# Order of the attention steps between the matmuls of a feed-forward block

## The chip, the core and the metric

The kernel runs on one core of a Trainium2 chip. The core has five engines that run side by side, each with its own queue of instructions in order: TensorE (matmuls, PE in the profile, its weight loads PEld), VectorE (DVE), ScalarE (ACT), GpSimd (POOL) and SyncE (SP), which issues transfers. Matmuls write to PSUM, an accumulator memory of eight banks of 512 fp32 numbers in each of 128 partitions. The other engines copy from there to SBUF, the working memory.

The metric is the device time of one execution in microseconds (us), as the median of several.

## What is computed

The inputs are q, k and v of shape (4, 8, 768, 64): four batches, eight heads, 768 positions of 64 numbers. A small matrix for each head, normalised by five rounds of exp and of division by its row and column sums, mixes the eight blocks of 96 positions of k and of v. Each block of q then attends to its mixed block, and a gated feed-forward block (FFN) follows on all 3072 tokens.

```
P = sort_net                                   # (4, 8, 8, 8), then 5 rounds:
    P = exp(P - max(P)); P = P / sum(P, -1); P = P / sum(P, -2)
k_sorted = einsum('bhij,bhjcd->bhicd', P, k_b)
v_sorted = einsum('bhij,bhjcd->bhicd', P, v_b)
scores = scale * q_b @ k_sb^T
attn = softmax(scores)
x = (attn @ v_sb)  -> (3072, 512)
g = x @ w_gate;  out = (silu(g) * (x @ w_val)) @ w_out
```

The weights w_gate and w_val are 512 x 1536, and w_out is 1536 x 512.

## The kernel before

**FFN stages.** The tokens are worked in eight half batches n = 0 to 7 of 384 tokens, two to a batch. In a stage, twelve blocks m of 128 hidden columns are computed one after another. `gate(n, m)` (L342) is four matmuls into the tile g_ps; ScalarE takes its tanh (th_sb, L354) and VectorE makes gs_sb of both (L356). `value(n, m)` (L360) is four matmuls into v_ps, which VectorE multiplies by gs_sb into h (L369). `outp(n, t3, part)` (L374) is the out projection of 128 tokens: three parts of four matmuls each into o_ps, then a copy to o_sb on ScalarE (L386) and a store from SyncE (L388). The out projection of stage n runs within stage n + 1, after blocks 3, 7 and 11; that of stage 7 stands at the end of the kernel.

**Attention steps.** They are put between the FFN's matmuls. The work for one unit u (a pair of heads and half of a batch's blocks; eight units to a batch) has these steps:

- `qk(b, u)` (L262): eight matmuls of 64 rows (L275), scores of two heads, into two PSUM banks, and one exp of both on ScalarE (L284) into `e_all`, a ring of eight slots.
- `av(b, u)` (L287): eight matmuls on the values (L295) into two banks. VectorE takes a reciprocal (L299) and scales (L301) into st.
- batches 0 and 1: `xtr` (L315), four transposes on TensorE (L312), and a copy on VectorE (L211) into xt, the input of the FFN; batches 2 and 3: `x_dma` (L323), a transposing transfer from SyncE.

Before the units of a batch its keys and queries are mixed in six chunks by `kq_chunk` (L227; 32 matmuls of 64 columns, L233, and one cast out of PSUM on VectorE or ScalarE, L211 or L213). The values of batch 1 are mixed in four chunks by `v_chunk` (L238; 16 matmuls on the 64 upper rows of vch, L245), and those of batches 2 and 3 together in eight by `v_pair_chunk` (L249; L255). For batches 2 and 3 the keys are mixed together as one pair ("p"), and the queries come by a transfer, `q_dma`.

**PSUM.** There are four tags. "gen" has three single banks, taken in turn by g_ps, v_ps and o_ps. "x" has one bank. "a" and "b" have two banks each: scores go to b, values to a, and chunks to b and a in turn. A tile can be taken only when the last reader of the tile before it in the same banks is done.

**Order.** From L498 on TensorE and GpSimd run in the order of the program text, and a planner orders ScalarE and VectorE. `merge` (L521) lays the attention steps between the FFN's steps: each FFN step has a cost in its list (0.65 for gate and value, 0.87 for a part of the out projection), and a side step is put in when the sum of the costs reaches its due time. The due times come from `spread` (L501), an even spacing between two fractions of the stage. `units` (L504) puts the steps in a fixed rotation: scores of one unit, values of the one before, then the transposes of the one before that.

**Start and loads.** GpSimd issues the loads in one order (L129 to L146): v, q and k of batch 0, then the weights w_gate and w_val in blocks of columns up to 1280, k and q of batch 1, the last weight blocks (columns 1280 to 1536, which are blocks 10 and 11), v of batch 1 and w_out. In the meantime GpSimd copies v into vch with its columns in another order (L120). TensorE runs matmuls on zeros at first (L396 to L402).

Of the kernel before, what the change touches and what calls it, by code (L numbers as in the profile page):

```python
# [9 lines left out]
FP32 = mybir.dt.float32  # L10
# [7 lines left out]
def kernel(  # L18
# [11 lines left out]
    nc = tc.nc  # L30

    B, H, S, D = q.shape
    NB = sort_net.shape[-1]
    C = S // NB
# [145 lines left out]
    def bank_tile(name, tag="gen"):  # L180
        return psum.tile([128, 512], FP32, name=name, tag=tag, bufs=3 if tag == "gen" else 1)
# [27 lines left out]
    def drain(eng, dst, src):  # L209
        if eng == "v":  # L210
            nc.vector.tensor_copy(dst, src)  # L211
        else:
            nc.scalar.copy(dst, src)  # L213
# [22 lines left out]
        drain(eng, dst[:, :, at:at + n], tp.transpose([0, 2, 1]))  # L236

    def v_chunk(b, at, n, eng, tag):  # L238
        rows = highr if b % 2 else lowr
        dst = vt_tile(b // 2)[:, b % 2]  # L240
        mix = vmix[b // 2][rows, b % 2].rearrange("p a b -> p (a b)")
        tp = chunk_tile("tv", n // 8, tag).rearrange("p (l n) -> p l n", n=H * NB)
        for ld in range(n):
            col = (at + ld) * C
            nc.tensor.matmul(tp[:, ld, :], lhsT=vch[rows, col:col + 128], rhs=mix,  # L245
                             start=True, stop=True)
        drain(eng, dst[:, :, at:at + n], tp[0:C].transpose([0, 2, 1]))
# [11 lines left out]
    es, sts, xts = {}, {}, {}  # L259
    ecount = [0]  # L260

    def qk(b, u, tag="b"):  # L262
        half, g = divmod(u, H2)
        k_sb, k_at, q_sb, q_at = ((kqts[b], 0, kqts[b], GI * C) if b < 2 else
                                  (kqts["p"], (b - 2) * GI * C, kqts["q"], (b - 2) * GI * C))
        if tag == "gen":
            pss = [bank_tile("qk"), bank_tile("qk")]
        else:
            wide = pair_tile("qk", tag).rearrange("p (two n) -> p two n", two=2)
            pss = [wide[:, 0], wide[:, 1]]  # L270
        for i4 in range(4):
            at = (g * NB + half * 4 + i4) * C
            for two in range(2):
                lo = two * D
                nc.tensor.matmul(pss[two][:, i4 * C:(i4 + 1) * C], lhsT=k_sb[lo:lo + D, k_at + at:k_at + at + 128],  # L275
                                 rhs=q_sb[lo:lo + D, q_at + at:q_at + at + C],
                                 start=True, stop=True)
        n = ecount[0] % 8
        ecount[0] += 2
        if tag == "gen":  # L280
            for two in range(2):
                nc.scalar.activation(e_all[:, n + two, 0:4 * C], pss[two][0:C, 0:4 * C], AF.Exp, scale=scale)
        else:
            nc.scalar.activation(e_all[:, n:n + 2, 0:4 * C], wide[0:C, :, 0:4 * C], AF.Exp, scale=scale)  # L284
        es[(b, u)] = [e_all[:, n, :], e_all[:, n + 1, :]]

    def av(b, u, tag="a"):  # L287
        half, g = divmod(u, H2)
        vt = vts[b // 2][:, b % 2].rearrange("p (h i) e -> p h i e", h=H)
        av_ps = pair_tile("av_ps", tag).rearrange("p (two n) -> p two n", two=2)  # L290
        o = av_ps[:, :, 0:4 * (D + 1)].rearrange("p two (i e) -> p two i e", e=D + 1)
        for two in range(2):
            e = es[(b, u)][two]
            for i4 in range(4):
                nc.tensor.matmul(o[:, two, i4, :], lhsT=e[:, i4 * C:i4 * C + 128],  # L295
                                 rhs=vt[:, 2 * g + two, half * 4 + i4, :],
                                 start=True, stop=True)
        r_sb = ssp.tile([C, 2, 4, 1], FP32, name="r_sb", tag="r")
        nc.vector.reciprocal(r_sb, o[0:C, :, :, D:D + 1])  # L299
        st = ssp.tile([C, 4, 2, D], BF16, name="st", tag="st")  # L300
        nc.vector.tensor_tensor(st.rearrange("p i two d -> p two i d"), o[0:C, :, :, 0:D],  # L301
                                r_sb.to_broadcast([C, 2, 4, D]), op=ALU.mult)
        sts[(b, u)] = st
# [11 lines left out]
    def xtr(b, u):  # L315
        half, g = divmod(u, H2)
        if g == 0:
            xts[(b, half)] = xtp.tile([128, H2, TW], BF16, name=f"xt{b}_{half}", tag="xt")
        x_ps = xt_tile("x", 1)[:, 0]
        x_to(x_ps, b, u)  # L320
        return xts[(b, half)][:, g, :], x_ps.rearrange("p a b -> p (a b)")

    def x_dma(b, u):  # L323
        half, g = divmod(u, H2)
        if g == 0:
            xts[(b, half)] = xtp.tile([128, H2, TW], BF16, name=f"xt{b}_{half}", tag="xt")
        nc.sync.dma_start_transpose(out=xts[(b, half)][:, g, :].rearrange("p (i c) -> p i c", c=C),
                                    in_=sts.pop((b, u)).rearrange("p i two d -> p (i two d)"))
# [5 lines left out]
    def q_dma(b):  # L334
        dst = kqt_tile("q")[:, (b - 2) * GI * C:(b - 1) * GI * C]
        nc.sync.dma_start_transpose(out=dst.rearrange("p (g s) -> p g s", g=H2), in_=q_scr[b - 2])
# [37 lines left out]
    def outp(n, t3, part):  # L374
        b, half = divmod(n, 2)
        h_w = h_tiles[n]
        if part == 0:
            o_tiles[n] = bank_tile("o_ps")
        o_ps = o_tiles[n]
        for m in range(part * 4, part * 4 + 4):  # L380
            nc.tensor.matmul(o_ps, lhsT=h_w[:, m, ts(t3, 128)], rhs=wo_sb[:, m, :],  # L381
                             start=(m == 0), stop=(m == NFC - 1))
        if part < 2:
            return
        o_sb = opool.tile([128, DM], FP32, name="o_sb", tag="o_sb")
        nc.scalar.copy(o_sb, o_ps)  # L386
        base = b * S + half * TW + t3 * 128
        nc.sync.dma_start(out=out[ds(base, 128), :], in_=o_sb)  # L388

    idle_ps = bank_tile("idle_ps", "x")  # L390

    def fill(tile, n):
        for _ in range(n):
            nc.tensor.matmul(tile, lhsT=warm_sb[:, 0:128], rhs=warm_sb, start=True, stop=True)  # L394

    for _ in range(82):  # L396
        nc.tensor.matmul(idle_ps[0:32, 0:32], lhsT=warm_sb[:, 0:32], rhs=warm_sb[:, 0:32],
                         start=True, stop=True)
    nc.tensor.matmul(idle_ps[:, 0:128], lhsT=ident[lowr, :],
# [98 lines left out]
    man = tc.manual_schedule(engines={ET.PE, ET.Pool})  # L498
    man.__enter__()

    def spread(steps, lo, hi):  # L501
        return [(lo + (hi - lo) * n / len(steps), f) for n, f in enumerate(steps) if f]

    def units(b, us):  # L504
        us = list(us)
        todo = []
        for n in range(len(us) + 2):
            todo.append((lambda u=us[n]: qk(b, u)) if n < len(us) else None)
            todo.append((lambda u=us[n - 1]: av(b, u)) if 1 <= n <= len(us) else None)
            if b < 2:  # L510
                todo.append((lambda u=us[n - 2]: drain("v", *xtr(b, u))) if 2 <= n else None)
            else:
                todo.append((lambda u=us[n - 1]: x_dma(b, u)) if 1 <= n <= len(us) else None)
        while todo[-1] is None:
            todo.pop()
        return todo

    def kqs(b):
        return [lambda n=n: kq_chunk(b, n * 16, 16, "vs"[n % 2], "ba"[n % 2]) for n in range(6)]

    def merge(main, side):  # L521
        total = sum(c for c, _ in main)
        done, k = 0.0, 0
        side = sorted(side, key=lambda t: t[0])
        for c, f in main:
            f()
            done += c
            while k < len(side) and side[k][0] * total <= done:
                side[k][1]()
                k += 1  # L530
        while k < len(side):
            side[k][1]()
            k += 1
# [14 lines left out]
    for s in range(4):  # L548
# [3 lines left out]
    q_cast(2)  # L552
    q_cast(3)
    both = slice(0, 128)
    merge(ffn(0), spread(units(0, range(4, 8)), 0.0, 0.6) + spread(kqs(1), 0.65, 1.0))
    merge(ffn(1), spread([lambda n=n: v_chunk(1, n * 16, 16, "sv"[n % 2], "ba"[n % 2]) for n in range(4)], 0.4, 0.55)
          + spread(units(1, range(4)), 0.55, 0.97))
    for s in range(4):
        copy_v(nc.gpsimd, 1, both, s)
    nc.vector.memset(kqt_tile("p")[:, 2 * GI * C:], 0.0)  # L560
    merge(ffn(2), spread(units(1, range(4, 8)), 0.0, 0.5) + spread(kqs("p"), 0.5, 0.95)
          + [(0.55, lambda: q_dma(2)), (0.7, lambda: q_dma(3))])
    merge(ffn(3), spread([lambda n=n: v_pair_chunk(1, n * 8, 8, "sv"[n % 2], "ba"[n % 2]) for n in range(8)], 0.0, 0.4)
          + spread(units(2, range(4)), 0.4, 0.85))
    merge(ffn(4), spread(units(2, range(4, 8)), 0.0, 0.85))
    merge(ffn(5), spread(units(3, range(4)), 0.0, 0.85))
    merge(ffn(6), spread(units(3, range(4, 8)), 0.0, 0.85))
    merge(ffn(7), [])
    for t3 in range(3):
        for part in range(3):  # L570
            outp(2 * B - 1, t3, part)
    man.__exit__(None, None, None)


# [28 lines left out]
```

## Time and profile before

| | |
|---|---|
| median of 11 runs | 259.67 us (258.97 to 260.85) |
| the profiled execution | 259.21 us |
| its span, first to last instruction | 257.1 us |
| granted TensorE clock in the span | 1.00 |
| gate, value, out projection matmuls (L346, L364, L381) | 76.6, 77.6 and 67.9 us busy |
| tanh (L354), mean of one | 490 ns |
| gs (L356) and h (L369), mean of one | 552 and 555 ns |
| exp of a unit (L284), mean of one | 801 ns |
| reciprocal and scaling of a unit (L299, L301), mean of one | 199 and 683 ns |
| copy of o_sb (L386), mean of one | 585 ns |
| store of o_sb, issue to landing | 2.1 us (median of 24) |

The profile is taken from one execution. A row names the line of the kernel, the engine, the operation and what is written and read; "x" is how many. The records of successive matmuls overlap[...]; the time that a matmul takes from the next is the distance between two starts. The chain of waits follows the end of the kernel back through what released each step.

### The profile page before, as it was taken

The page shows a single profiled execution, that of the slowest core. Times are in us where ns is not written, and L with a number is a line of the kernel's source. Part 1 is how long each engine was busy: PE and PEld are TensorE (multiplying, and loading weights), DVE is VectorE, ACT ScalarE, POOL GpSimd, SP SyncE. Part 2 cuts the span into 40 slices and gives each one's busy share as a digit, 9 for nine tenths or more (in the row PEclk, how much of TensorE's full clock was granted, in tenths as well). Part 3 has the DMA queues.
Part 4 walks back from the last instruction along what each step waited for, and adds up shares of the span by engine and source line. Part 5 has one row for each costly group of instructions (what it writes and reads, how often), then busy time and mean ns, then how long its engine had stood idle before and what let it go on. Part 6 is the DMA issues. An engine that isn't in the chain of part 4 may idle for free.

```text
span 257.1 us, 5985 instructions
## 1 busy us (share of the span) xinstructions
PE 245.7 (96%) x2525; PEld 140.5 (55%) x2525; DVE 163.1 (63%) x341; ACT 111.6 (43%) x186; POOL 51.9 (20%) x46
## 2 busy tenths in 40 slices
PE   3999998899999999999999999999999999999993
PEld 3385564555565565666555555555555555555541
DVE  6688796775586875847658457645864586456600
ACT  3967543334553533455543442344333443332311
POOL 7857520499369000000000000000000000000000
PEclk9999999999999999999999999999999999999999
DMA  6969999999999095110103110211121011100122
GB/s 102 212 96 169 198 223 212 195 227 191 204 181 140 2 156 134 41 43 0 43 15 89 41 56 18 73 42 40 33 74 41 15 59 58 54 18 25 42 84 83
DMA packets 37723, 23.99 MB, mean 93 GB/s; under 512 B 26048, under 2 KB 33728, under 8 KB 37184
## 3 DMA queue, kind: packets, MB, share of 16 engines
q0 software_dynamic: 21328, 14.16, 37.9%
q1 hardware_dynamic: 16368, 9.45, 12.7%
q8 instruction: 20, 0.33, 0.5%
q14 instruction: 7, 0.06, 0.1%
HBM read 28.32 MB, written 7.86 MB: 141 GB/s over the span
## 4 chain that ended last, share of the span: by engine, by line
PE 80%; DMA 13%; POOL 2%; DVE 1%; issue 1%; ACT 0%; ACTq 0%; POOLq 0%
PE o_ps L381 25%; PE v_ps L364 23%; PE g_ps L346 22%; DMA kq<-in_q_dram 6%; DMA kq<-in_k_dram 4%; DMA wv_sb<-in_moe_w_val_dram 3%; PE tkq L233 3%; PE qk L275 2%; PE av_ps L295 2%; PE tv L255 1%; DVE vt L211 1%; PE tv L245 1%; POOL kq L90 1%; POOL wg_sb L107 1%; PE x_ps L312 1%
## 5 line engine op out<-in xcount | busy, mean ns | idle before, releaser
L356 DVE SCALAR_TENSOR_TENSOR gs_sb<-th_sb,g_ps 128x384 bf16<-128x384 bf16 x96 | 53.0, 552 | 49.0 <-ACT th_sb L354 46.3
L364 PE MATMUL v_ps<-xt,wv_sb 128*128 128x384 bf16 x380 | 77.6, 326 | 0.2 <-DVE gs_sb L356 0.2
L346 PE MATMUL g_ps<-xt,wg_sb 128*128 128x384 bf16 x376 | 76.6, 326 | 0.1
L354 ACT ACTIVATE th_sb<-g_ps 128x384 bf16<-128x384 f32 x96 | 47.1, 490 | 60.4 <-PE g_ps L346 56.5
L381 PE MATMUL o_ps<-wo_sb,h 128*128 128x512 bf16 x288 | 67.9, 379 | 0.3 <-DVE h L369 0.3
L369 DVE SCALAR_TENSOR_TENSOR h<-v_ps,gs_sb 128x384 bf16<-128x384 f32 x96 | 53.3, 555 | 9.6 <-PE v_ps L364 1.9
L346 PEld LDWEIGHTS <-wg_sb 128*128 128x128 bf16 x376 | 35.0, 97 | 24.9 <-issue 1.5
L364 PEld LDWEIGHTS <-wv_sb 128*128 128x128 bf16 x380 | 33.9, 97 | 21.2 <-issue 0.2
L381 PEld LDWEIGHTS <-h 128*128 128x128 bf16 x288 | 26.8, 97 | 29.0 <-issue 0.7
L386 ACT COPY o_sb<-o_ps 128x512 f32<-128x512 f32 x24 | 14.0, 585 | 55.8 <-PE o_ps L381 55.8
L120 POOL COPY vch<-v 64x1536 bf16<-64x1536 bf16 (+1 forms) x10 | 28.0, 2848 | 20.8 <-DMA v<-in_v_dram 14.4
L284 ACT ACTIVATE e_all<-qk 96x768 bf16<-96x768 f32 x30 | 23.9, 801 | 9.3 <-PE qk L275 9.3
L301 DVE TENSOR_TENSOR st<-av_ps,r_sb 96x512 bf16<-96x512 f32 x32 | 21.9, 683 | 0.7
L295 PEld LDWEIGHTS <-e_all 96*128 96x128 bf16 x256 | 11.9, 98 | 6.0 <-ACT e_all L284 0.9
L295 PE MATMUL av_ps<-vt,e_all 96*128 96x65 bf16 x256 | 13.6, 194 | 0.4 <-ACT e_all L284 0.2
L211 DVE CAST vt<-tv 96x1024 bf16<-96x1024 f32 (+1 forms) x9 | 9.8, 1102 | 4.1 <-PE tv L255 2.5
L299 DVE RECIPROCAL r_sb<-av_ps 96x8 f32<-96x8 f32 x32 | 6.4, 199 | 8.7 <-PE av_ps L295 8.6
L213 ACT CAST vt<-tv 96x1024 bf16<-96x1024 f32 (+1 forms) x9 | 9.1, 1035 | 2.6 <-PE tv L245 1.3
L233 PE MATMUL tkq<-rmix,kq 128*64 128x64 bf16 x384 | 8.3, 197 | 1.7 <-issue 0.9
L394 PE MATMUL idle_ps<-warm_sb 128*128 128x512 bf16 x26 | 9.8, 489 | 0.0
L233 PEld LDWEIGHTS <-kq 128*64 128x64 bf16 x384 | 7.1, 113 | 4.5 <-issue 4.4
L213 ACT CAST kqt<-tkq 128x1024 bf16<-128x1024 f32 (+1 forms) x7 | 6.0, 894 | 5.2 <-PE tkq L233 5.0
(72 smaller groups left out, 131.0 us busy)
## 6 DMA issues: line engine op xcount, KB each, us to landing
out_dram<-o_sb SPq DMA_DIRECT2D x24, 256.0 KB, 2.1
v<-in_v_dram POOLq DMA_DIRECT2D x3, 768.0 KB, 12.4
kq<-in_q_dram POOLq DMA_DIRECT2D x2, 768.0 KB, 12.1
wg_sb<-in_moe_w_gate_dram POOLq DMA_DIRECT2D x6, 256.0 KB, 8.7
wv_sb<-in_moe_w_val_dram POOLq DMA_DIRECT2D x6, 256.0 KB, 9.3
wo_sb<-in_moe_w_out_dram POOLq DMA_DIRECT2D x1, 1536.0 KB, 23.6
kp<-in_k_dram POOLq DMA_DIRECT2D x2, 768.0 KB, 27.0
q_scr<-in_q_dram POOLq DMA_DIRECT2D x2, 768.0 KB, 18.4
```

The source lines that it names most:

```text
L120: eng.tensor_copy(dst, src.transpose([0, 2, 1]))
L213: nc.scalar.copy(dst, src)
L233: nc.tensor.matmul(tp[two * D:(two + 1) * D, lc, :], lhsT=kq_tiles[b][:, at + lc, :], rhs=rm[:, two, :], start=True, stop=True)
L284: nc.scalar.activation(e_all[:, n:n + 2, 0:4 * C], wide[0:C, :, 0:4 * C], AF.Exp, scale=scale)
L295: nc.tensor.matmul(o[:, two, i4, :], lhsT=e[:, i4 * C:i4 * C + 128], rhs=vt[:, 2 * g + two, half * 4 + i4, :], start=True, stop=True)
L301: nc.vector.tensor_tensor(st.rearrange("p i two d -> p two i d"), o[0:C, :, :, 0:D], r_sb.to_broadcast([C, 2, 4, D]), op=ALU.mult)
L346: nc.tensor.matmul(g_ps, lhsT=wg_sb[:, kc, ts(m, 128)], rhs=xt[:, kc, :], start=(kc == 0), stop=(kc == NKC - 1))
L354: nc.scalar.activation(th_sb, g_ps, AF.Tanh, scale=0.5)
L356: nc.vector.scalar_tensor_tensor(gs_sb, th_sb, 1.0, g_ps, op0=ALU.add, op1=ALU.mult)
L364: nc.tensor.matmul(v_ps, lhsT=wv_sb[:, kc, ts(m, 128)], rhs=xt[:, kc, :], start=(kc == 0), stop=(kc == NKC - 1))
L369: nc.vector.scalar_tensor_tensor(h_tiles[n][:, m, :], v_ps, 0.5, gs_tiles.pop(m), op0=ALU.mult, op1=ALU.mult)
L381: nc.tensor.matmul(o_ps, lhsT=h_w[:, m, ts(t3, 128)], rhs=wo_sb[:, m, :], start=(m == 0), stop=(m == NFC - 1))
```

## The change

Scores and exps are separate functions now, so that the exp can stand later than the scores. `units` takes due times in place of fractions. Two units form a group: scores of the first into b with their exp, and scores of the second into a, all at one due time; the exp of the second 1.3 later; values of the first (into b) 2.0 later and of the second (into a) 3.9 later; the transposes follow their values by 3.3, or the transposing transfer at once. `merge` compares due times with the sum of costs instead of a fraction of the total.

Key chunks run two at a time, the first into b with its cast on VectorE, the second into a with its cast on ScalarE. Of batch 1's six chunks, four move from the first FFN stage to the second. `v_chunk` for batch 1 multiplies all 128 rows, where the weights of the lower 64 are zero. The out projection of stages 2 to 6, and the first 128 tokens of that of stage 7, takes its bank from "x". The last 128 tokens are projected in two halves of 256 columns, one copied by ScalarE and one by VectorE, each stored on its own. 115 matmuls on zeros stand at the start in place of 82.

```diff
     def v_chunk(b, at, n, eng, tag):
-        rows = highr if b % 2 else lowr
+        rows = slice(0, 128) if b % 2 else lowr
...
-    def qk(b, u, tag="b"):
+    def scores(b, u, tag):
...
         if tag == "gen":
+            wide = None
             pss = [bank_tile("qk"), bank_tile("qk")]
...
+        return wide, pss
+
+    def exps(b, u, wide, pss):
         n = ecount[0] % 8
         ecount[0] += 2
-        if tag == "gen":
+        if wide is None:
...
+
+    def qk(b, u, tag="b"):
+        exps(b, u, *scores(b, u, tag))
...
-            o_tiles[n] = bank_tile("o_ps")
+            o_tiles[n] = bank_tile("o_ps", "x" if 2 <= n < 2 * B - 1 or n == 2 * B - 1 and t3 == 0 else "gen")
...
+    def out_halves(n, t3):
+        b, half = divmod(n, 2)
+        base = b * S + half * TW + t3 * 128
+        for part, eng in ((0, "s"), (1, "v")):
+            cols = slice(part * DM // 2, (part + 1) * DM // 2)
+            o_ps = bank_tile("o_ps")[:, 0:DM // 2]
+            for m in range(NFC):
+                nc.tensor.matmul(o_ps, lhsT=h_tiles[n][:, m, ts(t3, 128)], rhs=wo_sb[:, m, cols],
+                                 start=(m == 0), stop=(m == NFC - 1))
+            o_sb = opool.tile([128, DM // 2], FP32, name="oh_sb", tag="oh_sb")
+            drain(eng, o_sb, o_ps)
+            nc.sync.dma_start(out=out[ds(base, 128), cols], in_=o_sb)
...
-    for _ in range(82):
+    for _ in range(115):
...
-    def units(b, us):
+    def units(b, us, ats):
         us = list(us)
         todo = []
...
+        for n, at in enumerate(ats):
+            u, u2 = us[2 * n:2 * n + 2]
+            held = []
+            todo.append((at, lambda u=u, u2=u2, held=held: (qk(b, u, "b"), held.append(scores(b, u2, "a")))))
+            todo.append((at + 1.3, lambda u2=u2, held=held: exps(b, u2, *held[0])))
+            for w, tag, t in ((u, "b", 2.0), (u2, "a", 3.9)):
+                if b < 2:
+                    todo.append((at + t, lambda w=w, tag=tag: av(b, w, tag)))
+                    todo.append((at + t + 3.3, lambda w=w: drain("v", *xtr(b, w))))
+                else:
+                    todo.append((at + t, lambda w=w, tag=tag: (av(b, w, tag), x_dma(b, w))))
         return todo

-    def kqs(b):
-        return [lambda n=n: kq_chunk(b, n * 16, 16, "vs"[n % 2], "ba"[n % 2]) for n in range(6)]
+    def kqs(b, ats):
+        return [(at, lambda n=n: (kq_chunk(b, n * 32, 16, "v", "b"), kq_chunk(b, n * 32 + 16, 16, "s", "a")))
+                for n, at in enumerate(ats)]
+
+    def vs(f, size, ats):
+        return [(at, lambda m=m: f(1, m * size, size, "sv"[m % 2], "ba"[m % 2])) for m, at in enumerate(ats)]
...
-            while k < len(side) and side[k][0] * total <= done:
+            while k < len(side) and side[k][0] <= done:
...
-    merge(ffn(0), spread(units(0, range(4, 8)), 0.0, 0.6) + spread(kqs(1), 0.65, 1.0))
-    merge(ffn(1), spread([lambda n=n: v_chunk(1, n * 16, 16, "sv"[n % 2], "ba"[n % 2]) for n in range(4)], 0.4, 0.55)
-          + spread(units(1, range(4)), 0.55, 0.97))
+    kq1 = kqs(1, (11.8, 1.3, 5.2))
+    merge(ffn(0), units(0, range(4, 8), (0.0, 5.2)) + kq1[:1])
+    merge(ffn(1), kq1[1:] + vs(v_chunk, 16, (8.6, 9.4, 10.2, 11.0)) + units(1, range(4), (11.2, 15.0)))
...
-    merge(ffn(2), spread(units(1, range(4, 8)), 0.0, 0.5) + spread(kqs("p"), 0.5, 0.95)
-          + [(0.55, lambda: q_dma(2)), (0.7, lambda: q_dma(3))])
-    merge(ffn(3), spread([lambda n=n: v_pair_chunk(1, n * 8, 8, "sv"[n % 2], "ba"[n % 2]) for n in range(8)], 0.0, 0.4)
-          + spread(units(2, range(4)), 0.4, 0.85))
-    merge(ffn(4), spread(units(2, range(4, 8)), 0.0, 0.85))
-    merge(ffn(5), spread(units(3, range(4)), 0.0, 0.85))
-    merge(ffn(6), spread(units(3, range(4, 8)), 0.0, 0.85))
+    merge(ffn(2), units(1, range(4, 8), (0.0, 5.5)) + kqs("p", (13.0, 16.2, 19.4))
+          + [(13.0, lambda: q_dma(2)), (16.4, lambda: q_dma(3))])
+    merge(ffn(3), vs(v_pair_chunk, 8, [1.15 * n for n in range(8)]) + units(2, range(4), (9.8, 14.0)))
+    merge(ffn(4), units(2, range(4, 8), (0.0, 8.0)))
+    merge(ffn(5), units(3, range(4), (0.0, 8.0)))
+    merge(ffn(6), units(3, range(4, 8), (0.0, 8.0)))
     merge(ffn(7), [])
-    for t3 in range(3):
+    for t3 in range(2):
         for part in range(3):
             outp(2 * B - 1, t3, part)
+    out_halves(2 * B - 1, 2)
```

In the prediction g0 to g11 and v0 to v11 are the gate and value groups of a stage.

## The prediction

> **What bounds the kernel now.** I read the page's busy line first, then its chain of waits, then the PE timeline.
>
> ```profile
> PE 245.7 (96%) x2525; PEld 140.5 (55%) x2525; DVE 163.1 (63%) x341; ACT 111.6 (43%) x186; POOL 51.9 (20%) x46
> ...
> PE 80%; DMA 13%; POOL 2%; DVE 1%; issue 1%; ACT 0%; ACTq 0%; POOLq 0%
> ```
>
> TensorE carries 80% of the chain, and the loads carry the first 41 us. From 27.8 us on TensorE hardly stops, so a change pays only by what it takes off TensorE's issue or adds as a wait there. Records overlap, so I read a group's cost as the distance from its start to the next start (start, duration, engine, line):
>
> ```profile
> 195.32 0.81 PE L346 MATMUL g_ps<-xt,wg_sb 128*128 128x384 bf16 x4
> 196.06 0.34 PE L275 MATMUL qk<-kqtq,kqtp 64*128 64x96 bf16 x8
> 196.34 0.82 PE L364 MATMUL v_ps<-xt,wv_sb 128*128 128x384 bf16 x4
> 197.00 0.81 PE L346 MATMUL g_ps<-xt,wg_sb 128*128 128x384 bf16 x4
> 197.65 0.81 PE L364 MATMUL v_ps<-xt,wv_sb 128*128 128x384 bf16 x4
> ```
>
> A gate or value group costs 0.65 (197.00 to 197.65), but 0.74 when 64-row scores follow (195.32 to 196.06): entering costs 0.10. Groups before L233 (half the columns) and L245 (64 rows) show the same 0.10; groups before L295 and L312 do not. Leaving costs too, as the start of the kernel shows, where such groups stand together:
>
> ```profile
> 17.37 0.69 PE L233 MATMUL tkq<-rmix,kq 128*64 128x64 bf16 x32
> 18.00 0.39 PE L394 MATMUL idle_ps<-warm_sb 128*128 128x512 bf16 x1
> 18.31 0.95 PE L233 MATMUL tkq<-rmix,kq 128*64 128x64 bf16 x48
> 19.20 0.82 PE L394 MATMUL idle_ps<-warm_sb 128*128 128x512 bf16 x3
> 20.14 0.69 PE L275 MATMUL qk<-kqt 64*128 64x96 bf16 x24
> 20.76 0.39 PE L394 MATMUL idle_ps<-warm_sb 128*128 128x512 bf16 x1
> ```
>
> Three scores take 0.62, one alone 0.28 (196.06 to 196.34): each further one adds 0.17, so leaving costs 0.11. Key chunks: 48 matmuls 0.89, 32 take 0.63, so 32 more add 0.52, and leaving again costs 0.11. **Each excursion merged into another saves 0.10 + 0.11, say 0.20 us.**
>
> **Scores in pairs.** 28 units become 14 pairs. Two pairs lie in the first FFN stage, before a load that TensorE then waits for (below), and save nothing. 12 x 0.20 = **-2.40**.
>
> **Key chunks in twos.** For the pair of batches three excursions go: 3 x 0.20 = **-0.60**. Those of batch 1 are in the next item.
>
> **First FFN stage.** It waits for loads today:
>
> ```profile
> 41.40 0.14 issue
> ...
> 46.71 0.91 issue
> ```
>
> The chain view gives the query load's landing at 41.40, and 0.91 inside a key chunk with no releaser. The new order puts v10 before the first key chunks. v10 needs the last block of value weights:
>
> ```profile
> L107 POOL DMA_DIRECT2D wv_sb<-in_moe_w_val_dram x6: 755/788/833, 16.9 to 28.9; - x6
> ...
> DMA to landing us min/median/max: 5.2/9.3/15.7
> ```
>
> The last issue, at 28.9, has the longest landing: 44.6. With the 0.14 of the chain from landing to matmul, v10 starts at 44.7. From 27.8 the new order has 17 groups of 0.65, two pairs of scores of 0.55, four value steps of 0.26 and three transposes of 0.17 ahead of g10, 13.7 us (done 41.5), so whatever is saved there only lengthens the wait. From 44.7: v10 0.75, two key chunks 1.15, g11 0.65, transposes 0.17, v11 0.65 = 48.1. Four chunks move to the next stage, 2 x (1.15 + 0.10) = 2.50: equivalent end 50.6. Today the stage ends at 50.82 + 0.66 = 51.5. **-0.90**; 0 if the unexplained 0.91 comes back, -1.2 if that load lands earlier.
>
> **Values of batch 1 on all rows.** Today 61.40 to 61.97, 0.57 for 16 matmuls, plus 0.10 to enter. A rule speaks against this: the Trainium skill, "TensorEngine Tiling (Array Packing)", Row Tiling under Performance Considerations, advises row tiles for contractions up to 64, worth up to 2x. Given up, that would double four chunks, some +2. The row says nothing is lost: all 16 sit on one row group, and 0.57 less 0.11 for leaving is 29 ns each, no faster than the 32 ns of L295 with 96 rows (8 in 0.26). I take 16 x 31 ns = 0.50: 4 x (0.67 - 0.50) = **-0.68**.
>
> **A wait that the new order adds.** Sorting the steps of batch 1's first units gives, after the second out projection of that stage: scores of unit 2 into bank pair b, scores of unit 3 into a, then at once values of unit 1 (due 15.1 against 15.0), which also want a. They must wait until exp of unit 3 has read it, behind exp of unit 2 and the copy of o_ps. With 0 at the end of the projection's issue: copy 0.20 to 0.79 (it starts 0.20 after the next group in other stages), exp 2 from 0.7, exp 3 from 1.4 to 2.2 (0.80 each, overlapping by 0.1), values at 2.3 instead of 0.55. **+1.7**; 1.4 if the copy comes after the exps, 0 if the planner avoids it. Behind it TensorE's whole queue stands: the gates, hence tanh and VectorE.
>
> **Another one, before it.** The last value chunk (drained by VectorE from bank pair a) now stands one v_ps group ahead of the pair, whose second scores want a. Chunk data 0.2 after its end, cast 1.22, done 1.4; the scores come at 0.65 + 0.10 + 0.17 = 0.9. With VectorE 0.1 late: **+0.6** (0.2 to 1.1). These chunks also start near 59.7, when GpSimd's copies end (48.41 + 11.21 = 59.62): **+0.1**.
>
> **Values moved to stand after v_ps.** Today a value step between g_ps and v_ps puts 0.20 + 0.68 on VectorE ahead of h (L369); the third gen bank comes free late and TensorE loses 0.18, six times in the stages of batches 2 and 3 (155.40 to 156.23 is 0.83 for a 0.65 group). The new order has nearly all of them after v_ps or beside o_ps: about -1.0. Against it: v_pair chunk 7 now delays gs for v5 with no scores between (+0.4), and some 0.2 in batch 1's stages. **-0.4** (-1.0 to +1.0).
>
> **Out projection in the x bank.** In mid-kernel nothing: the bank has 8 us to drain. At the end outp(6) tile 2 and outp(7) tile 0 follow one another, both in the single x bank.
>
> ```profile
> 242.68 10.52 PE L381 MATMUL o_ps<-wo_sb,h 128*128 128x512 bf16 x48
> 245.47 0.58 ACT L386 COPY o_sb<-o_ps 128x512 f32<-128x512 f32 x1 [2.79 <-PE o_ps L381]
> ```
>
> Today the 13th matmul starts at 242.68 + 12 x 0.2162 = 245.27, in another bank. Then it must wait for the copy's end at 246.05, plus 0.05: **+0.83**. Nothing covers it.
>
> **Tail halves.** 24 matmuls of half the columns issue in the same 2.6. The last drain falls from 0.585 (ACT, 512 columns) to about 0.42 (VectorE; 96x512 took 0.685 and 96x1024 1.22, so 1.05 ns a column and 0.15 fixed). The store halves: the skill's "DMA: Bandwidth & Descriptors", Anatomy of one DMA, speaks against splitting: about 2.0 us of a DMA are fixed, and only bytes over 436 GB/s scale, so halving 256 KB saves 0.30 of an estimated 2.6. The rows say less: 256 KB land in 2.0 in all, the 8 KB load of p_sb in 1.7, so half the size saves about 0.15. By the page -0.47, by the rows **-0.32**.
>
> **33 more warm-up matmuls** take 33 x 29 ns = 0.96 inside the 1.1 us that TensorE waits for v: nothing.
>
> **Sum**: -2.40 - 0.60 - 0.90 - 0.68 + 1.7 + 0.7 - 0.4 + 0.83 - 0.32 = -2.07. The profiled execution took 259.21 (span 257.1 and 2.1 around it), so 257.1; the median shown is 259.67, 0.46 above, so **257.6**.
>
> **Rivals.** *The two new bank-a waits don't come* (ScalarE and VectorE are ordered by the planner, which may drain a earlier): 257.6 - 2.4 = 255.2. Against it: TensorE's order is fixed. *The first stage gains nothing*, the issue stall returning beside the load wait: +0.9 to 1.2, 258.6. *Slower, through ScalarE*: each pair puts two exps of 0.80 there within 2 us. Walked from g4: tanh 0.85 to 1.34, exp 1.24 to 2.04, exp 1.96 to 2.76, next tanh due at 2.75, because the pair gave TensorE 0.55 more. It just fits, with no margin; tanh late means gs late and v_ps without a bank, as the 0.65 groups run with 0.03 to spare. Where each of 12 pairs loses 0.3, it is +3.6: 261.2. It decides from 2.07 / 12 = 0.17 a pair. For it: value steps that upset VectorE cost just 0.18 today; against: ScalarE is 43% busy, and no exp costs TensorE anything visible today.
>
> **Numbers.** Forecast 0.44 (its own range 256.3 to 258.8), no waits 0.11, first stage 0.15, ScalarE 0.30. About 0.3% (0.8 us) is what can be told from no change here: faster 0.43 + 0.11 + 0.10 = 0.64; same 0.01 + 0.05 + 0.07 = 0.13; slower 0.23. The range leaves out half of the slower case and the best tenth: 255.5 to 260.8.
>
> **What would show it.** Scores in groups of 16 with starts 0.45 apart from the next; 0.10 missing ahead of half of them; a hole of 1.7 between o_ps and av_ps near 70 us, its releaser e_all; v10 at 44.7; a hole of 0.8 in the last o_ps row, released by o_sb; the last drain on VectorE. It is wrong if g_ps or v_ps groups after a pair stretch beyond 0.65 with gs or th as releaser, or if those holes are absent.

## The result, and the profile after

| | before | after |
|---|---|---|
| median, us | 259.89 (47 runs, 258.58 to 262.09) | 256.84 (12 runs, 255.09 to 260.28) |
| profiled execution, us | 259.21 | 257.23 |
| its span, us | 257.1 | 255.1 |

The changed kernel takes 0.9872 of the time, interval 0.9849 to 0.9894, with slow executions left out; the medians of all executions lie 3.05 us apart, where 2.07 less was forecast. The page's busy line and its chain of waits:

```profile
PE 239.9 (94%) x2570; PEld 143.5 (56%) x2570; DVE 159.7 (63%) x342; ACT 110.5 (43%) x186; POOL 52.0 (20%) x46
...
PE 76%; DMA 15%; POOL 3%; DVE 2%; ACT 1%; issue 1%; DVEq 0%; POOLq 0%
```

TensorE has 45 more matmuls and 5.8 us less busy time. ScalarE, which a rival made the new bound, has 1% of the chain. TensorE's timeline in the middle of the kernel (start, duration, engine, line) shows a pair:

```profile
193.78 0.81 PE L354 MATMUL g_ps<-xt,wg_sb 128*128 128x384 bf16 x4
194.53 0.52 PE L276 MATMUL qk<-kqtq,kqtp 64*128 64x96 bf16 x16
194.98 0.82 PE L372 MATMUL v_ps<-xt,wv_sb 128*128 128x384 bf16 x4
195.64 0.81 PE L354 MATMUL g_ps<-xt,wg_sb 128*128 128x384 bf16 x4
```

The group ahead of the pair takes 0.75 and the pair 0.45, as expected: with the 0.10 of entering, sixteen scores cost 0.55 where two separate units cost 0.76. Near 70 us stand the two waits that were worked out, here in the timeline of all engines; a bracket gives the idle time before a row and what ended it:

```profile
65.70 1.21 DVE L211 CAST vt<-tv 96x1024 bf16<-96x1024 f32 x1
66.22 0.34 PE L276 MATMUL qk<-kqt 64*128 64x96 bf16 x8
...
66.97 0.35 PE L276 MATMUL qk<-kqt 64*128 64x96 bf16 x8 [0.41 <-DVE vt L211]
...
71.50 0.51 PE L276 MATMUL qk<-kqt 64*128 64x96 bf16 x16
71.61 0.59 ACT L394 COPY o_sb<-o_ps 128x512 f32<-128x512 f32 x1 [3.01 <-PE o_ps L389]
72.09 1.51 ACT L289 ACTIVATE e_all<-qk 96x768 bf16<-96x768 f32 x2
73.65 0.41 PE L303 MATMUL av_ps<-vt,e_all 96*128 96x65 bf16 x8 [1.63 <-ACT e_all L289]
```

The second unit's scores come 0.75 after the first's instead of 0.17, behind the cast of the last value chunk. The values of unit 1 start 2.15 after the next pair instead of 0.45: ScalarE copies o_sb, then runs two exps, the second ends at 73.60, and only then is bank pair a free. At the end of the kernel, in the same view:

```profile
240.35 2.75 PE L389 MATMUL o_ps<-wo_sb,h 128*128 128x512 bf16 x12
243.14 0.59 ACT L394 COPY o_sb<-o_ps 128x512 f32<-128x512 f32 x1 [2.78 <-PE o_ps L389]
243.78 5.34 PE L389 MATMUL o_ps<-wo_sb,h 128*128 128x512 bf16 x24 [0.67 <-ACT o_sb L394]
...
250.87 1.70 SPq L409 DMA_DIRECT2D out_dram<-oh_sb  x2
251.78 0.42 DVE L211 COPY oh_sb<-o_ps 128x256 f32<-128x256 f32 x1 [10.16 <-PE o_ps L405]
```

The 13th matmul waits for the copy from the one x bank: 3.43 between the two starts instead of 2.59, 0.84 lost.

**Where the 3.05 us come from.** I cut each span at two rows: the start of the first value chunk of batch 1 (L245 near 60 us), and the start of the last v_ps matmul.

| stretch, us | before | after | difference |
|---|---|---|---|
| start to first value chunk, for equal work | 60.75 | 61.66 | +0.91 |
| first value chunk to last v_ps matmul, for equal work | 181.10 | 177.88 | -3.22 |
| last v_ps matmul to the end | 14.65 | 14.88 | +0.23 |

"Equal work": the new order puts that chunk ahead of one gate group, so 0.65 is taken from 61.40 before, and from 178.53 after. The sum, -2.08, is the difference of the spans less rounding. The middle is alike in every profile of the same order (178.53 in the changed kernel and in the four experiments that leave it as it is), but the start varies by over 2 us. The profiled execution of after is 0.39 above its median, that of before 0.68 below its own. The medians, -3.05, therefore leave about nothing for the start (-3.05 + 3.22 - 0.23 = -0.06).

### The profile page after: what moved, and what is told of

It reads as the page before. It is cut to its first block, busy times and chain, and to the rows that moved or that the text cites. A ratio compares the mean times of both kernels' runs of the same rounds, so it can differ in the third digit from the quotient of the medians.

```text
span 255.1 us, 6057 instructions
## 1 busy us (share of the span) xinstructions
PE 239.9 (94%) x2570; PEld 143.5 (56%) x2570; DVE 159.7 (63%) x342; ACT 110.5 (43%) x186; POOL 52.0 (20%) x46
## 4 chain that ended last, share of the span: by engine, by line
PE 76%; DMA 15%; POOL 3%; DVE 2%; ACT 1%; issue 1%; DVEq 0%; POOLq 0%
PE o_ps L389 23%; PE v_ps L372 22%; PE g_ps L354 21%; DMA wv_sb<-in_moe_w_val_dram 10%; DMA kq<-in_k_dram 5%; PE tkq L233 3%; PE av_ps L303 2%; PE qk L276 2%; PE tv L255 1%; PE o_ps L405 1%; POOL wg_sb L107 1%; ACT e_all L289 1%; DVE h L377 1%; PE x_ps L320 1%; POOL wv_sb L107 1%
## 5 line engine op out<-in xcount | busy, mean ns | idle before, releaser
L389 PE MATMUL o_ps<-wo_sb,h 128*128 128x512 bf16 x276 | 64.3, 379 | 0.7 <-ACT o_sb L394 0.7
L372 PEld LDWEIGHTS <-wv_sb 128*128 128x128 bf16 x380 | 35.2, 97 | 24.3 <-DMA wv_sb<-in_moe_w_val_dram 1.4
L120 POOL COPY vch<-v 64x1536 bf16<-64x1536 bf16 (+1 forms) x10 | 28.1, 2854 | 19.6 <-DMA v<-in_v_dram 19.6
L289 ACT ACTIVATE e_all<-qk 96x768 bf16<-96x768 f32 x30 | 22.7, 802 | 6.6 <-PE qk L276 6.6
L415 PE MATMUL idle_ps<-warm_sb 128*128 128x512 bf16 x26 | 8.2, 414 | 0.0
L211 DVE CAST kqt<-tkq 128x1024 bf16<-128x1024 f32 (+1 forms) x7 | 7.5, 1068 | 1.0 <-PE tkq L233 1.0
## 6 DMA issues: line engine op xcount, KB each, us to landing
out_dram<-o_sb SPq DMA_DIRECT2D x23, 256.0 KB, 2.0
wg_sb<-in_moe_w_gate_dram POOLq DMA_DIRECT2D x6, 256.0 KB, 9.5
wv_sb<-in_moe_w_val_dram POOLq DMA_DIRECT2D x6, 256.0 KB, 10.1
```

The lines of the kernel that those rows point to most:

```text
L120: eng.tensor_copy(dst, src.transpose([0, 2, 1]))
L372: nc.tensor.matmul(v_ps, lhsT=wv_sb[:, kc, ts(m, 128)], rhs=xt[:, kc, :], start=(kc == 0), stop=(kc == NKC - 1))
```

## The experiments

All edits are made on the changed kernel. "Middle" is the middle stretch as the profile has it, 178.53 in the changed kernel.

**Does the pairing pay 0.20 each?** First try: the second unit's scores at a due time of their own.

```diff
-            todo.append((at, lambda u=u, u2=u2, held=held: (qk(b, u, "b"), held.append(scores(b, u2, "a")))))
+            todo.append((at, lambda u=u: qk(b, u, "b")))
+            todo.append((at + 0.65, lambda u2=u2, held=held: held.append(scores(b, u2, "a"))))
```

> The changed kernel, but the scores of a pair's second unit stand one FFN step (0.65) behind those of the first, each an excursion of its own again; all other steps and banks as changed. Theory A (the gain is in merged excursions, 0.20 us each): 12 pairs outside the first stage lose it again, +2.4 against the changed kernel's 256.8, so about 259.2; in the trace single score groups of 0.28 with a 0.10 longer group before each. Theory B (the gain is in where the value steps stand, which relieves VectorE and the gen banks): scores apart change nothing, 256.8 within 0.5, and the 0.18 waits stay away.

Measured: 255.55 us, ratio to before 0.9846 (0.9816 to 0.9877), middle 177.87. Not slower, because the edit did something else as well. The four pairs due at 0.0 stayed together, since the first group brings the sum to 0.65 at once, and so did one near 130 us; only 7 of 12 were split: 19 excursions instead of 12, +1.47 at 0.21 each. But the values of unit 1 now stood ahead of the scores of unit 3, and the wait of 1.7 was gone. Split and wait had to be told apart, so I took the wait away alone:

```diff
-    merge(ffn(1), kq1[1:] + vs(v_chunk, 16, (8.6, 9.4, 10.2, 11.0)) + units(1, range(4), (11.2, 15.0)))
+    merge(ffn(1), kq1[1:] + vs(v_chunk, 16, (8.6, 9.4, 10.2, 11.0)) + units(1, range(4), (11.2, 15.7)))
```

> The changed kernel with the second pair of batch 1's first units due at 15.7 in place of 15.0, so that the values of unit 1 come before the scores that want bank pair a. Theory A (TensorE waits 1.6 there for two exps): the wait of av_ps on e_all near 73.6 us goes, -1.5 (to -1.7) against 256.8: 255.3. Rival (that wait gave VectorE and the loads time that is then missing): it is spread over later waits, -0.5 or less.

and then split the pairs on top of it (the edit of the first try with 0.7 for 0.65; 11 of the 12 came apart):

> late_pair, with the scores of the second unit 0.7 behind those of the first in every pair, so that neither kernel has the wait of av_ps on e_all. Theory A (0.20 for each excursion): 12 pairs outside the first stage are 24 score groups again, +2.4 of excursions, less the 0.58 that the scores of batch 1's first pair wait for the value cast in late_pair: +1.8 against late_pair's 255.6, 257.4; in the trace 0.10 more ahead of each and 0.28 for each. Theory B: 255.6 within 0.5.

Measured: 255.59 (0.9826, 0.9795 to 0.9857), middle 177.24, for the wait taken away; 255.92 (0.9854, 0.9803 to 0.9905), middle 178.42, with the pairs split as well. TensorE's timeline without the wait:

```profile
71.00 0.42 PE L303 MATMUL av_ps<-vt,e_all 96*128 96x65 bf16 x8
71.26 0.81 PE L354 MATMUL g_ps<-xt,wg_sb 128*128 128x384 bf16 x4
72.01 0.78 PE L276 MATMUL qk<-kqt 64*128 64x96 bf16 x16
72.72 0.82 PE L372 MATMUL v_ps<-xt,wv_sb 128*128 128x384 bf16 x4
```

The values go ahead of the pair and wait for nothing. What is left is 0.26: the pair takes 0.71 instead of 0.45. The middle falls by 1.29 of the 1.70. Splitting adds 11 excursions in this stretch, 11 x 0.21 = 2.31, and takes away waits of 0.46 (0.58 less the 0.11 of leaving), 0.26, 0.24 and 0.32, with a new one of 0.17: -1.11. That makes +1.20; the two middles differ by +1.18, where +1.8 was expected. The medians, 0.33 apart with overlapping intervals, can't tell the two kernels apart; the middle can. **The price of an excursion is shown there, and so is the price of the pairs' own waits**: two units back to back ask for both bank pairs at once.

**Is the wait at the end the x bank's?**

```diff
-            o_tiles[n] = bank_tile("o_ps", "x" if 2 <= n < 2 * B - 1 or n == 2 * B - 1 and t3 == 0 else "gen")
+            o_tiles[n] = bank_tile("o_ps", "x" if 2 <= n < 2 * B - 1 else "gen")
```

> The changed kernel with the out projection of the last stage's first 128 tokens in a gen bank in place of x. Theory A: the wait of o_ps on the copy o_sb (0.67 by the record, 0.82 by starts) goes, and with nothing behind it to hide in the end comes 0.8 earlier: 256.0. Rival (the wait moves to the last drain or store): 256.8 within 0.3.

Measured: 255.70 (0.9841, 0.9813 to 0.9870). The last stretch falls from 14.88 to 14.04. TensorE's timeline of this kernel:

```profile
241.07 7.93 PE L389 MATMUL o_ps<-wo_sb,h 128*128 128x512 bf16 x36
248.84 2.78 PE L405 MATMUL o_ps<-wo_sb,h 128*128 128x256 bf16 x24
```

The same 36 matmuls take 7.77 to the next start; in the changed kernel it is 248.96 - 240.35 = 8.61. The 0.84 is the one bank's, shown.

**What are the halves worth?** The last 128 tokens in one piece again (the loop at the end over three tiles, `out_halves` gone):

> The changed kernel with the last 128 tokens projected and stored whole. By the rows: last drain 0.17 and store 0.15 longer, the end 0.3 later behind the last value group. By the fixed cost of a transfer alone: the store no longer, 0.17 later.

Measured (one run): 256.25, last stretch 15.44 instead of 14.88. So the halves save 0.56. The store of 256 KB landed 2.01 after its issue (250.90 to 252.91), the last one of 128 KB in 1.71: 0.30. The drain falls from 0.585 to 0.42: 0.17. The remaining 0.1 lies after the last landing (1.22 to the end of the span instead of 1.13); what it is was not looked for.

**Values of batch 1 on the upper 64 rows again** (`rows = highr if b % 2 else lowr`):

> The changed kernel with the values of batch 1 mixed on the upper 64 rows again. Prediction's row: a chunk is 0.57 and enters for 0.10 in place of 0.47 and nothing, 4 x 0.20 = +0.8 of groups between the first value chunk and the last value group, less what of the 0.58 wait of the scores behind the last chunk it covers. By the tiling rule (64 rows run two at once): -0.9.

Measured (one run): 257.48, middle 179.15, +0.62. TensorE's timeline, first of this kernel and then of the changed one:

```profile
61.29 0.64 PE L245 MATMUL tv<-vmix,vch 64*128 64x64 bf16 x16
61.86 0.82 PE L354 MATMUL g_ps<-xt,wg_sb 128*128 128x384 bf16 x4
62.62 0.64 PE L245 MATMUL tv<-vmix,vch 64*128 64x64 bf16 x16
```

```profile
61.66 0.63 PE L245 MATMUL tv<-vmix,vch 128*128 128x64 bf16 x16
62.12 0.81 PE L354 MATMUL g_ps<-xt,wg_sb 128*128 128x384 bf16 x4
62.77 0.63 PE L245 MATMUL tv<-vmix,vch 128*128 128x64 bf16 x16
```

On 64 rows a chunk costs 0.57 and the group before the next one 0.76; on all rows 0.46 and 0.65. All sixteen matmuls sit on the same 64 rows here, and they come no faster than on 128; no run spread them over both halves.

**Are the six waits of 0.18 gone because the values stand after v_ps?** For batches 2 and 3 I put them between g_ps and v_ps again:

```diff
-            for w, tag, t in ((u, "b", 2.0), (u2, "a", 3.9)):
+            for w, tag, t in ((u, "b", 2.0), (u2, "a", 3.9)) if b < 2 else ((u, "b", 1.7), (u2, "a", 3.0)):
```

> The changed kernel, but the value steps of batches 2 and 3 stand between g_ps and v_ps again (1.7 and 3.0 after their scores), where most of them stood before. Theory G (there the reciprocal and scaling go ahead of h on VectorE and a gen bank comes free 0.18 late): 12 steps of the stages of the second half of batch 2 and of batch 3 lose 0.18 each, +2.2 between the first value chunk of batch 1 and the last value group, 257.2 to 259 in all. Rival (the waits before came from exps and o_ps copies, not from where the value step stands): within 0.4 of the changed kernel.

Measured (one run): 255.16, middle 178.34, -0.19 against the changed kernel. My theory expected +2.2 and is refuted. The timelines of all engines say why. The kernel before, and then this experiment:

```profile
154.09 0.81 PE L364 MATMUL v_ps<-xt,wv_sb 128*128 128x384 bf16 x4
...
155.03 0.68 DVE L301 TENSOR_TENSOR st<-av_ps,r_sb 96x512 bf16<-96x512 f32 x1
...
155.40 0.81 PE L364 MATMUL v_ps<-xt,wv_sb 128*128 128x384 bf16 x4
...
155.63 0.54 DVE L369 SCALAR_TENSOR_TENSOR h<-v_ps,gs_sb 128x384 bf16<-128x384 f32 x1
...
156.23 0.81 PE L346 MATMUL g_ps<-xt,wg_sb 128*128 128x384 bf16 x4
```

```profile
143.39 0.81 PE L372 MATMUL v_ps<-xt,wv_sb 128*128 128x384 bf16 x4
...
144.32 0.68 DVE L309 TENSOR_TENSOR st<-av_ps,r_sb 96x512 bf16<-96x512 f32 x1
...
144.69 0.42 PE L303 MATMUL av_ps<-vt,e_all 96*128 96x65 bf16 x8
...
144.93 0.54 DVE L377 SCALAR_TENSOR_TENSOR h<-v_ps,gs_sb 128x384 bf16<-128x384 f32 x1
144.95 0.81 PE L372 MATMUL v_ps<-xt,wv_sb 128*128 128x384 bf16 x4
```

The scaling stands ahead of h in both, and h ends late, at 156.17 and 145.47. Before, the third group after that v_ps wants its bank at 156.05 and starts at 156.23. In the experiment the second unit's values stand in between with 0.26, so the third group comes at 145.60, when the bank is free; without them it would have come at 145.34 and waited. So a value step between g_ps and v_ps costs 0.18 only where no other step follows within the next groups. That is a reading of the two traces; no run tried it alone.

**Does the load of the value weights set the first stage?** Two key chunks more ahead of block 10:

```diff
-    kq1 = kqs(1, (11.8, 1.3, 5.2))
-    merge(ffn(0), units(0, range(4, 8), (0.0, 5.2)) + kq1[:1])
+    kq1 = kqs(1, (11.0, 11.6, 1.3))
+    merge(ffn(0), units(0, range(4, 8), (0.0, 5.2)) + kq1[:2])
```

(in the line after it, `kq1[2:]` for `kq1[1:]`)

> The changed kernel with two of batch 1's three pairs of key chunks ahead of g10 and v10 (due 11.0 and 11.6), the third in the second stage at 1.3. Theory A (TensorE idles 2.4 us ahead of g10 and v10 for the last weight blocks, and key chunks whose q and k land earlier would fill it): 2.4 of matmuls move into the idle time, less about 0.5 by which v10 gets later: -1.9 against 256.8, 254.9. Rival (the key chunks themselves wait for q, which lands 0.9 before the gate weights, and their casts for VectorE and ScalarE): -0.5 or less.

Measured: 256.93 (0.9885, 0.9855 to 0.9914): no gain. Its profiled execution lost the TensorE clock ahead of the first stage (below) and couldn't tell, so I ran the edit again with 82 warm-ups, and beside it 82 warm-ups alone and three edits together (82 warm-ups, the later pair, the last stage in gen):

> The changed kernel with 82 warm-up matmuls, as before. Theory C (115 of them bring the full clock at 6 to 8 us instead of 11.7; the 11 big matmuls then end at 10, TensorE idles 1.5 us until p_bf, and in about half of the executions the clock is withdrawn for 6.8 us, mean clock 0.985 to 0.987): with 82 the mean clock is 0.997 or more in every execution, as in the kernel before, and the median falls by about half of the 0.9 us between executions of the two kinds, 256.8 to 256.3. Rival (the withdrawal comes from the stage that waits for weights, where TensorE idles too): executions at 0.987 stay, and the time does not move by more than 0.3.

> late_pair, tail_gen and warm82 in one. If the three waits are separate and each on the path: -1.5, -0.8 and -0.5 against 256.8, 254.0. If the early gain is lost to the weight loads again (v10 cannot start before they land), only what lies behind v10 counts, -1.5 and -0.8: 254.5.

> combo82 with the key chunks of kq_fill. With the full clock the first stage comes early enough to wait for the weights, so the chunks fill idle time: -1.5 against combo82. Rival (its key chunks wait for q and for each other's casts, as kq_fill's clock-disturbed profile can't exclude): within 0.5 of combo82.

Measured: 256.94 (0.9858, 0.9811 to 0.9905) for 82 alone; 254.40 (0.9773, 0.9731 to 0.9814) for the three; 254.39 (0.9784, 0.9740 to 0.9827) with the key chunks. The fill again brings nothing. TensorE's timeline of the last kernel shows what takes over:

```profile
54.63 0.81 PE L372 MATMUL v_ps<-xt,wv_sb 128*128 128x384 bf16 x4
56.41 2.76 PE L389 MATMUL o_ps<-wo_sb,h 128*128 128x512 bf16 x12 [0.96 <-DMA wo_sb<-in_moe_w_out_dram]
59.01 0.81 PE L354 MATMUL g_ps<-xt,wg_sb 128*128 128x384 bf16 x4
59.66 0.81 PE L372 MATMUL v_ps<-xt,wv_sb 128*128 128x384 bf16 x4
60.57 0.61 PE L245 MATMUL tv<-vmix,vch 128*128 128x64 bf16 x15
```

The first out projection waits for w_out, whose last transfer landed at 56.37, and the first value chunk for GpSimd's copies of v, which ended at 60.51. They begin when v of batch 1 has landed, at 49.25 here: four of 2.85 (L120). **Up to 60 us one load after another sets the pace, and work saved there only lengthens the next wait.** In the three profiles with 82 warm-ups just named, the value chunk starts 0.05 to 0.06 after the end of these copies.

**The version that beats both.** The three edits, the first pair of batch 1 one group later and the second pair of batch 2 one later, so that their own waits go too:

```diff
-    merge(ffn(1), kq1[1:] + vs(v_chunk, 16, (8.6, 9.4, 10.2, 11.0)) + units(1, range(4), (11.2, 15.0)))
+    merge(ffn(1), kq1[1:] + vs(v_chunk, 16, (8.6, 9.4, 10.2, 11.0)) + units(1, range(4), (11.715, 15.7)))
...
-    merge(ffn(3), vs(v_pair_chunk, 8, [1.15 * n for n in range(8)]) + units(2, range(4), (9.8, 14.0)))
+    merge(ffn(3), vs(v_pair_chunk, 8, [1.15 * n for n in range(8)]) + units(2, range(4), (9.8, 14.8)))
```

> combo82 with the first pair of batch 1 one gate group later (11.715), so that its scores do not wait 0.58 for the value cast, and the second pair of batch 2 behind the whole out projection (14.8), so that its scores do not wait 0.32 for the scaling of unit 1. Theory A (each wait seen at a group's start is on the path): -0.9 between the first value chunk of batch 1 and the last value group, against combo82's 254.4: 253.5. Rival (VectorE, later relieved, hands the waits on): 254.4 within 0.3.

Measured: **253.74** (0.9768, 0.9728 to 0.9808), middle 176.87, 0.36 less than with three edits. Waits of 0.47 and 0.31 are gone, and one of 0.45 is new, since this v_ps now stands behind a late gs, in TensorE's timeline:

```profile
132.72 0.81 PE L354 MATMUL g_ps<-xt,wg_sb 128*128 128x384 bf16 x4
133.81 0.48 PE L372 MATMUL v_ps<-xt,wv_sb 128*128 128x384 bf16 x2 [0.28 <-DVE gs_sb L364]
```

Its interval lies clear of the changed kernel's but overlaps with that of the three edits.

## Why the prediction was right, and where it was not

Direction and range held, and the likeliest case was the right one, 0.8 us too high. By its own steps:

- **Pairs, -2.40.** Right: 0.21 an excursion, 12 of them.
- **Key chunks, -0.60.** About right by the rows: in the middle six chunks of 0.63 with an entry of 0.10 each became three pairs of 1.13 with one entry each, -0.69. Not tried on their own.
- **First FFN stage, -0.90.** About nothing between the medians of all executions; -0.58 if only the six of the changed kernel with the fuller clock are taken (256.32, below). The step named the right load, and its sum behind that load held: 3.37 from the start of v10 to the end of v11, and 46.50 to 49.87 in the trace. But it took one execution's landing, 44.6, for a constant; in the profile of after that load landed at 46.45, and v10 waited 0.97 for it. Of the eight profiles of changed kernels with an undisturbed clock, the five in which it landed by 44.95 start the first value chunk at 59.59 to 60.16, the three in which it landed from 45.51 on at 60.57 to 61.66; before it was 60.75, with a landing at 44.57. The rival "first stage gains nothing" is near the medians' size, but its reason, an issue stall of 0.9, was not seen again; the cause of that stall stays open.
- **Values on all rows, -0.68.** Right: 0.46 to 0.47 and no 0.10, -0.72 within the middle. Undone, it costs +0.62, with a wait beside it shortened by 0.13.
- **Bank pair a, +1.7 and +0.6.** Measured 1.70 and 0.58. The rival in which the two waits don't come is refuted; taking the first away gives 1.29 back.
- **Values moved, -0.4.** This term was mis-sized, by 1.2. Waits of before that were counted: six of 0.18. Waits that stood in the same trace and went as well: 0.29 at 76.41 (g_ps to av_ps), 0.49 at 119.20 (value chunk to o_ps, h late), 0.26 at 126.11 (scores to v_ps, gs late), 0.18 at 139.23. That is 2.3 instead of 1.0. New are 0.23 at 129.33, 0.32 at 132.55 and 0.12 at 138.61, 0.67 where 0.6 was expected. Net -1.64. The reason given for the six, the position after v_ps, is at best half of it. Two of the waits that were passed over, in TensorE's timeline of before:

```profile
119.20 0.61 PE L255 MATMUL tv<-vmix,vch 128*128 128x128 bf16 x8
120.14 1.02 PE L381 MATMUL o_ps<-wo_sb,h 128*128 128x512 bf16 x4 [0.33 <-DVE h L369]
...
126.11 0.34 PE L275 MATMUL qk<-kqtq,kqtp 64*128 64x96 bf16 x8
126.65 0.65 PE L364 MATMUL v_ps<-xt,wv_sb 128*128 128x384 bf16 x3 [0.19 <-DVE gs_sb L356]
```

- **The middle as a whole**: 12 x 0.21 = 2.52, 0.69 and 0.72 saved, 2.28 of waits for bank pair a added, 1.64 saved: -3.29, against -3.22 measured. Nothing large is missing.
- **x bank, +0.83, and halves, -0.32.** Measured +0.84 and -0.56. For the store I set the page's rule against an 8 KB load and took the load. The rule of the Trainium skill, "DMA: Bandwidth & Descriptors", Anatomy of one DMA, was right in its size term, 0.30 (2.01 against 1.71). Its fixed 2.0 us is stated for transfers that GpSimd issues; these stores are issued by SyncE, and there 256 KB land in 2.01 in all.
- **Warm-ups, nothing.** Nothing in the median (256.94 with 82, 256.84 with 115), but not without effect: see below.
- **Slower through ScalarE.** Refuted: no gate or value group behind a pair waits for ScalarE. After the 0.23, 0.32 and 0.12 between 129 and 139 us, no step is late until the out projection at the end.

The two wrong sizes, values moved (1.2 too small a gain) and first stage (0.3 to 0.8 too large), partly cancel, and the halves add 0.24. That the total came so near its likeliest value is partly luck. The direction and the range are not: with either of the two errors alone the total would be 256.0 or 258.1, both within the range.

## What to carry to other kernels

Before pricing a reorder, list every group on the bounding engine that lasts longer than its matmuls, with its releaser: each such wait may go or move, and a list of only the largest or of one pattern missed half of them here. Steps put back to back save the cost of the switch between them, but ask for all their banks at one moment; check for each bank who read it last, and what else stands in that reader's queue. Where loads set the pace, follow the chain to its last load before crediting any saving, and take a landing time from more than one execution.

## What the hardware showed that was not expected

**More warm-up can lose the clock.** Two profiles by window: start and end, length, then the busy time of PE, PEld, DVE, ACT and POOL with their instructions, the granted clock, the DMA share and GB/s. First the key-chunk experiment with 115 warm-ups, then 82 alone:

```profile
6.00:12.00 6.00, 3.44 (x32) 1.62 (x28) 4.30 (x20) 5.82 (x7) 5.61 (x2) 1.00 1.01 211
12.00:20.00 8.00, 8.00 (x183) 6.71 (x180) 4.25 (x7) 5.26 (x8) 3.55 (x6) 0.57 0.67 108
```

```profile
6.00:12.00 6.00, 5.24 (x29) 1.99 (x29) 4.30 (x20) 5.87 (x7) 5.56 (x2) 1.00 1.01 212
12.00:20.00 8.00, 7.86 (x266) 6.07 (x264) 6.26 (x9) 5.61 (x9) 3.71 (x6) 1.00 0.66 108
```

With 115 the eleven large fill matmuls end sooner (in 2.55 us instead of 4.37), and TensorE idles longer before the first real work, which waits for VectorE's p_bf. TensorE's timeline of the same two profiles:

```profile
11.32 0.76 PE L429 MATMUL w_ps<-ident,p_bf 32*64 32x32 bf16 x16 [2.30 <-DVE p_bf L203]
```

```profile
11.29 0.76 PE L429 MATMUL w_ps<-ident,p_bf 32*64 32x32 bf16 x16 [0.45 <-DVE p_bf L203]
```

In the first of the two profiles the clock then drops to half, from 12.85 to 19.68 us (mean 0.50 there): 0.57 over 8 us is 6.9 us at half speed, and 183 matmuls are done instead of 266. The first value group of the FFN came at 30.43 instead of 28.08. The Trainium skill, "TensorE: Matmul & The Clock Gate", Part 1, describes a gate with two rates, half and full, and a window of 3413 ns; two such windows are 6.83 us, which is what this trace shows. The profiles sort by the idle time: of the nine with 115 warm-ups the five that idled 1.93 to 2.31 us lost the clock (mean 0.985 to 0.992), and the four that idled 1.33 to 1.60 kept it (0.998 or more); with 82 it was 0.48 at most, and none lost it. So a warm-up that ends early can be worse than a shorter one. That the idling is the reason fits all of them, but no run changed it alone.

In 20 of 45 executions with 115 warm-ups the mean clock was 0.984 to 0.987; with 82 it was so in 1 of 24, and in 1 of the 33 runs of the kernel before that stood beside the experiments. Among the twelve runs of the changed kernel, the six at the low clock have a median of 257.08, the other six 256.32. That 82 lowers the median is nevertheless not shown: the landing of the loads moves it more (256.94 with 82 alone).

**Loads land at different times.** The load of v of batch 1 landed between 48.10 and 50.52 us in the fourteen profiles, with the same loads issued in the same order. That is as much as the largest term of the prediction's sum; its cause was not looked for.
